# A late layernorm apply moved to ScalarE, and PSUM slots behind the loop taken from a written list

## Chip, cores and metric

The kernel runs on one core of a Trainium2 chip. The engines are PE (TensorE matmuls; PEld are its weight loads), DVE (VectorE), ACT (ScalarE), POOL (GpSimd) and SP (SyncE, which here only issues DMAs). The metric is the device time of one execution in microseconds (us); less is better. The kernel before takes 275.93 us, the median of 3 runs (275.52 to 276.19).

## What is computed

One transformer block on x of 2048 rows and 640 columns in bf16: layernorm, a linear attention with a softmax feature map, a residual, a second layernorm, a gated feed-forward layer of width 1536, and a residual. Cut to what matters:

```python
def _A_ref(x, wqkv, w_phi, wo):            # 32 heads of 20 columns
    q, k, v = qkv[0], qkv[1], qkv[2]       # of x @ wqkv
    phi_q = concat([softmax(q @ w_phi), softmax(-(q @ w_phi))])
    phi_k = concat([softmax(k @ w_phi), softmax(-(k @ w_phi))])
    kv = einsum("bhsf,bhsd->bhfd", phi_k, v)
    z  = einsum("bhsf->bhf", phi_k)
    o  = (phi_q @ kv) / (phi_q . z + 1e-6)
    return o @ wo
def _B_ref(x, w_gate, w_up, w_down):
    return (gelu(x @ w_gate) * (x @ w_up)) @ w_down
h  = x + _A_ref(_layernorm(x), ...)
h2 = h + _B_ref(_layernorm(h), ...)
```

## The kernel before

The 2048 rows are 16 tiles of 128. All of the kernel stands under a manual schedule: each engine runs its instructions in the order of the source, and waits only for what it needs.

**Front (to about 20 us).** The first tiles are normalised and projected, and w_phi is folded into the key weights. Tiles 0 and 1 are a special case (`CT`): what goes into their columns of `LN1T[0]` at first is x less its mean; 1/std is applied later, as the scale of the ScalarE evictions. For tile 1 the list `va[1]` holds four columns: minus the mean (0), the sum of squares (1), the variance plus eps (2) and 1/std (3).

**The loop over 16 passes (lines 463 to 514).** Pass t makes the keys of tile t (`k_tile`: PE into `pk`, two ScalarE exponentials into `E`), the values of tile t+4 (`v_mm`, `v_ev`), the layernorm of tile t+6 (`ln_ap`), and the norm of the keys (`k_norm`: a sum and a reciprocal on DVE, two products `vt`, on POOL and DVE). Passes 10 to 14 also fold w_phi into the query weights (`fold`, PE into `wa`, a ScalarE cast into `Wq2`). Some passes run `kv_tile` for tiles gathered up to then; it adds to `kvp` in PSUM. Since the query matmuls need tiles 0 and 1 normalised in full, their columns of `LN1T[0]` are written once more, by a layernorm and a transposing DMA of SP: tile 1 in pass 10 (`ln_a(1)`, line 396, on DVE) and tile 0 in pass 12 (`ln_ap(0, on_act=True)`, line 144, on ScalarE). Pass 13 has SP issue the loads of `Wo` and `Wg`. Pass 15 makes the first four query groups `q_mm(0..3)` (PE into `pq`, ScalarE exponentials into `Eq`); the first needs tiles 4 to 7 alone, the second is the first to read `LN1T[0]`. Behind the loop `kv_tile(13..15)` ends `kvp`, and `kv_mask` (lines 358 and 360, DVE) writes the masked `KV` from it.

**Behind the loop.** The other query groups `q_mm(q)` to `q_mm(q+8)` (q is 4) are woven by hand with the attention of tiles 0 to 2: `attn_a` (PE into two tiles `ab`, copied out by ScalarE and DVE), `attn_b` to `attn_b3`, `attn_t` and `attn_e` (transposes), `attn_c` (PE into `po`), `attn_d`. Then `weave` runs units of the feed-forward layer (`gate_up`: ten matmuls into `gu`, a gelu on ScalarE from its first half, a product on DVE from its second; `down`: twelve matmuls into `pd`) with pieces of later tiles' attention between them. The first `weave` is of tiles 0 and 1, the second of tiles 2 and 3, and so on.

**PSUM.** The kernel divides PSUM into eight banks. In the loop a pool of three slots of two banks (`psG`, banks 0 to 5) serves `pk`, `pv`, `wa` and `pq` in turn, and `kvp` has the last two banks. The last four tiles of the three slots are the query groups 0 to 3: group 1 in banks 4 and 5, group 2 in banks 2 and 3, group 0 and then group 3 in banks 0 and 1. Behind the loop the pools are closed and `psG2` opens, four slots of two banks. In the kernel as compiled, its 63 tiles get the slots (slot i is banks 2i and 2i+1) 0, 3, 2, 1, 3, 2, 0, 3, 2, 3, 1 and so on, to a last `0, 1, 3, 2, 0, 1, 3, 2`; the first is the `pq` of `q_mm(q)`, the next two are `ab` of tile 0, and the last is the `gu` of the twelfth `gate_up` of the second `weave`. Right behind that unit `split()` closes the pool and opens `psB`, eight slots of one bank, which hand out banks 0, 7, 6, 1, 5, 4, 3, 2; the first is `pd` of the unit that follows, `down(0, 2, 0)`. A pool of eight single-bank slots begins at bank 0 whatever was there before. All these pools are opened with `reuse_waits="tile"`: a new tile waits for all that read the old tile in its place. This goes by whole tiles: in the compiled kernel the `ab` tile in bank 5 behind the split waits for the gelu of the last `gu`, though that gelu reads bank 4 alone.

Of the kernel before, what the change touches and what calls it, by code (L numbers as in the profile page):

```python
# [8 lines left out]
BF16 = mybir.dt.bfloat16  # L9
F32 = mybir.dt.float32  # L10
ALU = mybir.AluOpType
ACTF = mybir.ActivationFunctionType
AX = mybir.AxisListType
PSUM = bass.MemoryType.PSUM
# [3 lines left out]
def kernel(  # L18
# [12 lines left out]
    nc = tc.nc  # L31
    P = 128
# [42 lines left out]
    ps_cm = ExitStack()  # L75
    psG = ps_cm.enter_context(tc.tile_pool(name="psG0", bufs=4, space=PSUM, reuse_waits="tile"))
# [4 lines left out]
    x_sb = [const.tile([P, 4, D], BF16, name=f"x_sb{b}") for b in range(NB)]  # L81
# [19 lines left out]
    def small(pool, shape, name, bufs=3):  # L101
        return pool.tile(shape, F32, name=name, bufs=bufs)

    def gtile(name):
        return psG.tile([P, 2, 512], F32, name=name, tag="G")

    def ln_stats(pool, tiles, tag, act=True, between=None, log=False):

# [43 lines left out]
    def transpose_to(dst, src, on_pe, on_dve=False):  # L152

        if on_pe:
            tp = psG.tile([P, 16, P], BF16, name="tp", tag="G")
            for c in range(NC):
                nc.tensor.transpose(tp[:, c, :], src[:, c * P:(c + 1) * P], ident)  # L157
            (nc.vector.tensor_copy if on_dve else nc.scalar.copy)(dst, tp[:, 0:NC, :])  # L158
        else:
            nc.sync.dma_start_transpose(dst, src)  # L160
# [4 lines left out]
    LN1T = [LN1F.bitcast(BF16).rearrange("p (b c n) -> p b c n", b=NB, c=NC)[:, b] for b in range(NB)]  # L165
# [56 lines left out]
    def fold(WT, W2, quarters, ds=range(NC)):  # L222


        n, w = (2, QF) if quarters else (1, HD)
        runs = []
        for c in range(NC):
            lo, hi = H0[c] * Dh, (H0[c] + NH[c]) * Dh
            for r in range(2 * n):
                a, b = max(lo, r * w), min(hi, (r + 1) * w)  # L230
                if a < b:
                    runs.append((r // n, r, c, a, b))
        runs.sort()
        for d in ds:
            wa = gtile("wa")
            wr = wa.rearrange("p u (q x) -> p (u q) x", q=n)
            for i, (u, r, c, a, b) in enumerate(runs):
                nc.tensor.matmul(wr[:, r, a - r * w:b - r * w], lhsT=WT[:, c, d * P:(d + 1) * P],
                                 rhs=BD[:, c].rearrange("p a b -> p (a b)")[:, a - H0[c] * Dh:b - H0[c] * Dh],
                                 start=(i == 0 or runs[i - 1][0] != u),  # L240
                                 stop=(i + 1 == len(runs) or runs[i + 1][0] != u), skip_group_check=True)
            dst, src = W2[:, d, :].rearrange("p (u f) -> p u f", u=2), wr[:, :, 0:w]
            if quarters:
                dst = W2[:, d, :].rearrange("p (c r f) -> p r c f", c=NC, r=4)
                src = src.rearrange("p r (c f) -> p r c f", c=NC)
            if d in (QA if quarters else KA):
                nc.scalar.copy(dst, src)
            else:
                nc.vector.tensor_copy(dst, src)
# [19 lines left out]
    def ln_ap(t, on_act=False, on_pe=False):  # L269
        ln = (ln_act if on_act else ln_dve)(p1, "1", *lnp[t])  # L270
        if on_pe:
            lnp[t] = ln
        else:
            transpose_to(LN1T[t // 4][:, :, t % 4 * P:(t % 4 + 1) * P], ln, False)
# [15 lines left out]
    def v_mm(t, us=(0, 1)):  # L290
        if 0 in us:
            pv[t] = gtile("pv")
        proj(pv[t], t, Wv, us)
# [10 lines left out]
    def v_ev(t):  # L304
        nc.scalar.activation(vS[t % 8][:, :, 0:Dh].rearrange("p (u h) f -> p u h f", u=2),
                             pv[t][:, :, 0:HD].rearrange("p u (h f) -> p u h f", f=Dh), ACTF.Copy,
                             scale=lnp[t][2] if t in CT else 1.0)
# [5 lines left out]
    def k_tile(t):  # L313
        pk = gtile("pk")
        proj(pk, t, Wk2, rows=t == 0)
        Ek[t] = ev.tile([P, 2, D], BF16, name="E", bufs=8)
        for s in range(2):
            nc.scalar.activation(Ek[t][:, s, :].rearrange("p (u f) -> p u f", u=2), pk[:, :, 0:HD],  # L318
                                 ACTF.Exp, scale=((lnp[t][2], nrstd[t]) if t in CT else (1.0, -1.0))[s])
# [25 lines left out]
    def kv_tile(t):  # L345

        for s in range(2):
            for c in range(NC):
                i, h, n = SLOT[c]
                for r in range(4):  # L350
                    f0, h0 = r * QF + c * 32, r * QH + h
                    nc.tensor.matmul(kvp[QUAD[r], s * SL + i:s * SL + i + n, :],  # L352
                                     lhsT=Ek[t][:, s, f0:f0 + 32], rhs=Vt[t][:, s, h0:h0 + n, :],
                                     start=(s == c == t == 0), stop=(t == NT - 1), skip_group_check=True)
# [10 lines left out]
    def q_mm(j, part=(0, 1)):  # L365

        if 0 in part:
            pqs[j] = gtile("pq")
        for i, bc in enumerate(QG[j]):
            if i not in part:  # L370
                continue
            b, c = divmod(bc, NC)
            for kc in range(NC):
                nc.tensor.matmul(pqs[j][:, i, :], lhsT=Wq2[:, kc, c * P:(c + 1) * P], rhs=LN1T[b][:, kc, :],  # L374
                                 start=(kc == 0), stop=(kc == NC - 1))

    def q_exp(j, signs=(0, 1)):
        for s in signs:
            nc.scalar.activation(Eq[j][:, :, s, :], pqs[j][:, 0:len(QG[j])], ACTF.Exp, scale=(1.0, -1.0)[s])  # L379
# [13 lines left out]
    def ln_a(t):  # L393

        ln = p1.tile([P, D], BF16, name="ln1", bufs=3)
        nc.vector.tensor_scalar(ln, x_sb[0][:, t, :], va[t][:, 0:1], va[t][:, 3:4], op0=ALU.add, op1=ALU.mult)
        return ln

    def xc_a(t):
# [6 lines left out]
    va = {1: p1.tile([P, 4], F32, name="va1")}  # L406
# [56 lines left out]
    for t in range(NT):  # L463
        if t == T3:
            ps_cm.close()
            psG = ps_cm.enter_context(tc.tile_pool(name="psG", bufs=3, space=PSUM, reuse_waits="tile"))
            psK = ps_cm.enter_context(tc.tile_pool(name="psK", bufs=1, space=PSUM, reuse_waits="tile"))
            kvp = psK.tile([P, 2 * SL, VC], F32, name="kvp")
        k_tile(t)
        if t == 0:  # L470
            ln_ap(6)
        if t in FQ:
            fold(WqT, Wq2, True, [i for i, f in enumerate(FQ) if f == t])
        for i in KVG.get(t, ()):
            kv_tile(i)
        for j in range(len(QT)):
            if t == QT[j]:
                q_mm(j)
                q_exp(j)
                for i in KVQ.get(j, ()):  # L480
                    kv_tile(i)
        if 0 < t < NT - 4:
            v_mm(t + 4)
        if t > 0 and t + 6 < NT:
            ln_ap(t + 6, on_act=True)
        if 0 < t < NT - 4:
            v_ev(t + 4)
        if t % 2 == 0 and t + 8 < NT:
            ln_st(t + 8, t + 9)
        k_norm(t)  # L490
        load_T(WqT, 0, *[i for i, f in enumerate(LQ) if f == t])
        if t == 10:
            transpose_to(LN1T[0][:, :, P:2 * P], ln_a(1), False)
        if t == 12:
            ln_ap(0, on_act=True)
        if t == 7:
            nc.gpsimd.memset(kmask[QUAD[0]], 1.0)
            for k, lo, n, base in ((3, 0, 2, 0), (2, 6, 3, 12)):
                m = kmask[QUAD[0], lo:lo + 6].rearrange("p (k n) -> p k n", k=k)
                nc.gpsimd.affine_select(out=m, in_=m, pattern=[[4, k], [-Dh, n]],  # L500
                                        compare_op=ALU.is_ge, fill=0.0, base=base, channel_multiplier=1)
                nc.gpsimd.affine_select(out=m, in_=m, pattern=[[-4, k], [Dh, n]],
                                        compare_op=ALU.is_ge, fill=0.0, base=Dh - 1 - base, channel_multiplier=-1)
        if t == 8:
            nc.gpsimd.memset(KV, 0.0)
        if t == 9:
            for r in (1, 2, 3):
                nc.sync.dma_start(kmask[QUAD[r]], kmask[QUAD[0]])
        if t == 11:
            nc.gpsimd.tensor_copy(KV[:, 0, :, KC - 1], kmask)  # L510
            nc.gpsimd.tensor_copy(KV[:, 1, :, 0], kmask)
        if t == 13:
            nc.sync.dma_start(Wo, wo_v)
            nc.sync.dma_start(Wg, wg_v)
# [5 lines left out]
    p1_cm.__exit__(None, None, None)  # L520
    ps_cm.close()
    ps_cm = ExitStack()
    psG = ps_cm.enter_context(tc.tile_pool(name="psG2", bufs=4, space=PSUM, reuse_waits="tile"))


    p2 = ctx.enter_context(tc.tile_pool(name="p2", bufs=1, reuse_waits="tile"))
# [334 lines left out]
```

## Time and profile before

| | us |
|---|---|
| median of 3 runs (lowest, highest) | 275.93 (275.52, 276.19) |
| the profiled execution, its own time | 276.65 |
| its span, first to last instruction | 274.7 |
| PE busy in the span | 268.2 |
| DVE, ACT, POOL busy | 174.2, 141.1, 96.6 |

The profile is of one execution, which took 276.65 us; its instructions span 274.7, and 1.95 lie around them. The granted TensorE clock was 0.999 of full speed. A timeline row has start, length, engine (`SPq` is SP's queue), line, operation, tiles as out<-in, shapes and a count; several like instructions that follow one another are one row. What stands in brackets is the engine's idle time ahead of the row and what ended it.

### The profile page before, as it was taken

How to read it: one execution, taken by the hardware profiler on the slowest of the kernel's cores; microseconds unless marked ns; L12 is line 12 of the kernel's file. 1: busy time of each engine (PE TensorE's matmuls, PEld its weight loads, DVE VectorE, ACT ScalarE, POOL GpSimd, SP SyncE). 2: the span in 40 equal slices, each digit the busy share in tenths (PEclk: the TensorE clock that was granted, in tenths of full speed). 3: DMA queues.
4: the chain of work that ended last, by engine and by line, in shares of the span. 5: the costliest groups of instructions: out<-in, count | busy, mean ns of one | idle time of the engine just before them, and what ended most of it. 6: DMA issues, size and time to landing. Idle time of an engine off the chain costs nothing.

```text
span 274.7 us, 7230 instructions
## 1 busy us (share of the span) xinstructions
PE 268.2 (98%) x2978; PEld 171.7 (63%) x2995; DVE 174.2 (63%) x332; ACT 141.1 (51%) x241; POOL 96.6 (35%) x219
## 2 busy tenths in 40 slices
PE   7999999999899999999999999999999999999996
PEld 4776777774455887788754554675554576444574
DVE  5879999997586776675459873346976333333332
ACT  5789897787689755374534445212445510223100
POOL 4248999775012227365321552101165300000000
PEclk9999999999999999999999999999999999999999
DMA  7963637577079021323111232110214111000011
GB/s 190 221 218 71 66 60 91 78 152 312 2 246 328 5 50 37 85 51 73 33 43 49 26 70 51 40 58 1 66 32 64 35 48 50 24 0 0 2 48 48
DMA packets 42400, 21.46 MB, mean 78 GB/s; under 512 B 35200, under 2 KB 40576, under 8 KB 42368
## 3 DMA queue, kind: packets, MB, share of 16 engines
q1 hardware_dynamic: 41712, 20.98, 31.9%
q8 instruction: 23, 0.38, 0.6%
q10 hardware_dynamic: 656, 0.03, 0.2%
q14 instruction: 9, 0.07, 0.1%
HBM read 10.18 MB, written 2.62 MB: 47 GB/s over the span
## 4 chain that ended last, share of the span: by engine, by line
PE 73%; issue 0%; ACT 0%; DVE 0%
PE gu L697 38%; PE pd L716 19%; PE po L637 8%; PE pq L374 5%; PE ab L565 2%; PE tp L157 0%; ACT Eq L379 0%; DVE y L719 0%
## 5 line engine op out<-in xcount | busy, mean ns | idle before, releaser
L703 DVE TENSOR_TENSOR GT<-gu,g 128x512 bf16<-128x512 f32 (+1 forms) x60 | 34.4, 580 | 47.3 <-PE gu L697 38.5
L700 ACT ACTIVATE g<-gu 128x512 bf16<-128x512 f32 (+1 forms) x60 | 30.7, 512 | 63.6 <-PE gu L697 62.7
L697 PE MATMUL gu<-LN2T,Wg 128*128 128x512 bf16 (+1 forms) x289 | 61.2, 335 | 0.6
L697 PE MATMUL gu<-LN2T,Wu 128*128 128x512 bf16 (+1 forms) x300 | 61.8, 336 | 0.0
L716 PE MATMUL pd<-Wd,GT 128*128 128x320 bf16 (+2 forms) x396 | 53.5, 295 | 0.0
L716 PEld LDWEIGHTS <-GT 128*128 128x128 bf16 x396 | 37.9, 98 | 14.6 <-DVE GT L703 0.2
L697 PEld LDWEIGHTS <-Wu 128*128 128x128 bf16 x300 | 29.4, 98 | 22.6
L697 PEld LDWEIGHTS <-Wg 128*128 128x128 bf16 x300 | 28.6, 98 | 20.8
L285 PEld LDWEIGHTS <-LN1T 128*128 128x128 bf16 x290 | 27.7, 98 | 11.2 <-DMA LN1T<-ln 0.9
L719 DVE TENSOR_TENSOR y<-pd,x_sb 128x320 bf16<-128x320 f32 (+2 forms) x29 | 13.9, 480 | 29.4 <-PE pd L716 29.4
L333 POOL TENSOR_TENSOR vt<-vS,rs 128x672 bf16<-128x672 bf16 x22 | 29.2, 1349 | 7.5 <-DVE rs L329 7.2
L637 PE MATMUL po<-Wo,oT 128*128 128x320 bf16 x160 | 24.4, 299 | 0.0
L285 PE MATMUL pk<-Wk,LN1T 128*128 128x320 bf16 x160 | 24.2, 299 | 0.0
L374 PE MATMUL pq<-LN1T,Wq 128*128 128x512 bf16 x94 | 22.9, 379 | 1.2 <-ACT Eq L379 0.9
L325 DVE TENSOR_REDUCE sk<-E 128x64 f32<-128x1280 bf16 x16 | 22.9, 1430 | 0.0
L379 ACT ACTIVATE Eq<-pq 128x1024 bf16<-128x1024 f32 (+1 forms) x26 | 20.0, 828 | 3.3 <-PE pq L374 3.3
L285 PE MATMUL pv<-Wv,LN1T 128*128 128x320 bf16 x130 | 19.8, 299 | 0.4 <-DMA LN1T<-ln 0.3
L637 PEld LDWEIGHTS <-oT 128*128 128x128 bf16 x160 | 15.5, 98 | 7.0 <-ACT oT L158 0.5
L318 ACT ACTIVATE E<-pk 128x640 bf16<-128x640 f32 x28 | 18.2, 706 | 3.0 <-PE pk L285 2.9
L614 DVE TENSOR_TENSOR tt<-AB,w 128x1280 bf16<-128x1280 f32 x12 | 17.8, 1486 | 1.0 <-POOL w L607 0.9
L144 ACT ACTIVATE ln<-x_sb,v,rstd 128x640 bf16<-128x640 bf16 x14 | 12.9, 920 | 10.8 <-POOL v L676 10.3
L374 PEld LDWEIGHTS <-Wq 128*128 128x128 bf16 x100 | 9.4, 98 | 10.6 <-PE kvp L352 0.5
(114 smaller groups left out, 288.7 us busy)
## 6 DMA issues: line engine op xcount, KB each, us to landing
out_dram<-y SPq DMA_DIRECT2D x15, 160.0 KB, 1.8
Wg<-in_B_w_gate_dram SPq DMA_DIRECT2D x1, 1920.0 KB, 10.2
Wu<-in_B_w_up_dram SPq DMA_DIRECT2D x1, 1920.0 KB, 8.5
Wd<-in_B_w_down_dram SPq DMA_DIRECT2D x2, 960.0 KB, 11.8
x_sb<-in_A_x_dram SPq DMA_DIRECT2D x2, 640.0 KB, 6.5
Wo<-in_A_wo_dram SPq DMA_DIRECT2D x1, 800.0 KB, 5.6
x_sb<-in_A_x_dram SPq DMA_DIRECT2D x4, 160.0 KB, 3.4
Wv<-in_A_wqkv_dram SPq DMA_DIRECT2D x2, 320.0 KB, 4.5
```

The costliest lines, as they stand in the source:

```text
L285: nc.tensor.matmul(ps[:, u, 0:HD], lhsT=lnT(t, c), rhs=W[:, c, u * HD:(u + 1) * HD], start=(c == 0), stop=(c == NC - 1))
L318: nc.scalar.activation(Ek[t][:, s, :].rearrange("p (u f) -> p u f", u=2), pk[:, :, 0:HD], ACTF.Exp, scale=((lnp[t][2], nrstd[t]) if t in C ...
L325: nc.vector.reduce_sum(sk, Ek[t].rearrange("p s (h f) -> p (s h) f", f=Dh), axis=AX.X)
L333: eng.tensor_tensor(vt[:, s], vS[t % 8], rs[:, s * H:(s + 1) * H, None].to_broadcast([P, H, VC]), ALU.mult)
L374: nc.tensor.matmul(pqs[j][:, i, :], lhsT=Wq2[:, kc, c * P:(c + 1) * P], rhs=LN1T[b][:, kc, :], start=(kc == 0), stop=(kc == NC - 1))
L379: nc.scalar.activation(Eq[j][:, :, s, :], pqs[j][:, 0:len(QG[j])], ACTF.Exp, scale=(1.0, -1.0)[s])
L614: nc.vector.tensor_tensor(tt.rearrange("p s (h f) -> p s h f", f=Dh), num, w[:, :, :, None].to_broadcast([P, 2, H, Dh]), ALU.mult)
L637: nc.tensor.matmul(pos[u], lhsT=st[t][:, c, :], rhs=Wo[:, c, u * HD:(u + 1) * HD], start=(c == 0), stop=(c == NC - 1))
L697: nc.tensor.matmul(gu[i][:, 0:n], lhsT=W[:, c, f * P:(f + 1) * P], rhs=LN2T[b][:, c, a0:a1], start=(c == 0), stop=(c == NC - 1))
L700: nc.scalar.activation(g[:, 0:n], gu[0][:, 0:n], ACTF.Gelu_apprx_tanh)
L703: nc.vector.tensor_tensor(st[b, "g", f][:, a0:a1], gu[1][:, 0:n], g[:, 0:n], ALU.mult)
L716: nc.tensor.matmul(ps, lhsT=st[b, "g", f][:, tl * P:(tl + 1) * P], rhs=Wd[:, f, f0:f1], start=(f == 0), stop=(f == NF - 1))
```

## The change

`ln_a(1)` goes from DVE to ScalarE and, with its transposing DMA, from pass 10 to pass 13, ahead of that pass's loads of `Wo` and `Wg`. ScalarE's form needs minus the mean times 1/std as a bias; one POOL multiply in pass 8 puts it into `va[1][:, 2:3]`. Behind the loop four pools of one slot each take the place of the pool of four, and a written list `ROT` says which of them each tile gets.

```diff
-    def gtile(name):
-        return psG.tile([P, 2, 512], F32, name=name, tag="G")
+    psP = None
+
+    def gtile(name, shape=[P, 2, 512], dt=F32):
+        return (psP[ROT.pop(0)] if psP else psG).tile(shape, dt, name=name, tag="G")
...
-            tp = psG.tile([P, 16, P], BF16, name="tp", tag="G")
+            tp = gtile("tp", [P, 16, P], BF16)
...
         ln = p1.tile([P, D], BF16, name="ln1", bufs=3)
-        nc.vector.tensor_scalar(ln, x_sb[0][:, t, :], va[t][:, 0:1], va[t][:, 3:4], op0=ALU.add, op1=ALU.mult)
+        nc.scalar.activation(ln, x_sb[0][:, t, :], ACTF.Identity, bias=va[t][:, 2:3], scale=va[t][:, 3:4])
         return ln
...
-        if t == 10:
-            transpose_to(LN1T[0][:, :, P:2 * P], ln_a(1), False)
         if t == 12:
             ln_ap(0, on_act=True)
+        if t == 13:
+            transpose_to(LN1T[0][:, :, P:2 * P], ln_a(1), False)
...
         if t == 8:
+            nc.gpsimd.tensor_tensor(va[1][:, 2:3], va[1][:, 0:1], va[1][:, 3:4], op=ALU.mult)
             nc.gpsimd.memset(KV, 0.0)
...
-    psG = ps_cm.enter_context(tc.tile_pool(name="psG2", bufs=4, space=PSUM, reuse_waits="tile"))
+    psP = [ps_cm.enter_context(tc.tile_pool(name=f"psP{i}", bufs=1, space=PSUM, reuse_waits="tile")) for i in range(4)]
+    ROT = [2, 3, 0, 1, 3, 0, 2, 3, 0, 3, 1, 3, 1, 2, 0, 3, 1, 0, 2, 3, 0,
+           1, 2, 3, 0, 1, 2, 0, 1, 3, 2, 0, 1, 2, 3, 0, 1, 2, 3, 0, 1, 2,
+           3, 0, 1, 3, 0, 2, 1, 3, 0, 2, 1, 3, 0, 2, 1, 3, 0, 2, 1, 3, 0]
```

`ROT` has 63 entries. Entry by entry it is the order in which `psG2` hands out its slots in the kernel before, with 0 written for 2 and 2 for 0.

## Prediction

> **What bounds the kernel now.** I read the busy times first: PE 268.2 of 274.7 us, DVE 174.2, ACT 141.1. So a change counts by what it does to PE's gaps. Next the waits of PE itself from 20 us on:
>
> ```profile
> PE pq L374 <- ACT Eq L379: 0.9, 1, 0.9
> PE pv L285 <- DMA LN1T<-ln: 0.3, 1, 0.3
> ```
>
> The reader is to see that PE waits twice for other engines after the first 20 us. The 0.3 is a transpose near 47 us, which the change leaves alone. The 0.9 stands at the end of the loop, and the timeline there shows it whole:
>
> ```profile
> 62.07 1.14 PE L352 MATMUL kvp<-vt,E 128*32 128x42 bf16 x120
> ...
> 63.14 5.57 PE L374 MATMUL pq<-LN1T,Wq 128*128 128x512 bf16 x24
> ...
> 65.51 1.94 ACT L379 ACTIVATE Eq<-pq 128x1024 bf16<-128x1024 f32 x2 [1.40 <-PE pq L374]
> ...
> 67.67 2.92 ACT L379 ACTIVATE Eq<-pq 128x1024 bf16<-128x1024 f32 x4 [0.22 <-PE pq L374]
> ...
> 68.64 1.14 PE L352 MATMUL kvp<-vt,E 128*32 128x42 bf16 x120
> ...
> 70.09 0.68 DVE L360 TENSOR_TENSOR KV<-kvp,kmask 128x504 bf16<-128x504 f32 x1
> 70.23 0.10 PEld L374 LDWEIGHTS <-Wq 128*128 128x128 bf16 x1 [0.55 <-PE kvp L352]
> 70.64 1.24 PE L374 MATMUL pq<-LN1T,Wq 128*128 128x512 bf16 x4 [0.86 <-ACT Eq L379]
> ...
> 71.81 0.47 PE L565 MATMUL ab<-KV,Eq 32*128 32x44 bf16 x40
> ```
>
> The first pq behind the loop sits in slot 0, where query group 3 was; it starts at 70.64, 0.05 after the last exponential of that group (67.67 + 2.92 = 70.59). From there PE runs on without a wait to the end (the chain of waits is PE's own from 70.64), and DVE, ACT and POOL follow it. So a time won or lost on PE here is kept, until PE meets a new wait. The place for one is the split, where the pool of eight single banks opens:
>
> ```profile
> 132.92 0.71 PE L697 MATMUL gu<-LN2T,Wu 128*128 128x256 bf16 x5
> ...
> 133.35 0.76 ACT L700 ACTIVATE g<-gu 128x256 bf16<-128x256 f32 x2
> ...
> 133.46 3.42 PE L716 MATMUL pd<-Wd,GT 128*128 128x320 bf16 x24
> ...
> 133.75 0.81 DVE L703 TENSOR_TENSOR GT<-gu,g 128x256 bf16<-128x256 f32 x2 [1.37 <-ACT g L700]
> ```
>
> The reader is to see the order: PE begins pd at 133.46, right behind the last gu, while that gu is still to be read, by ACT until 133.35 + 0.76 = 134.11 and by DVE until 133.75 + 0.81 = 134.56.
>
> **The layernorm: off DVE.** Line 396 goes, at 51.85 a row of 1.00 us. DVE's products then come up to 1.0 earlier, and PE doesn't wait for DVE or POOL in the loop: 0.
>
> The Trainium skill ("ScalarE: Activation LUTs", section "Rules for kernel authors") speaks against this move: adds and multiplies belong on VectorE, not on ScalarE. The rows say the same by half: the same shape takes 0.445 on DVE at line 149, but 1.00 in this place, and 0.94 on ACT. By the rule the move would cost 0.5 us, by the rows of this place it costs none; in the sum it is neither, since neither engine holds PE here.
>
> **The layernorm: onto ACT.** The nearest row is tile 0's, of the same shape one pass before:
>
> ```profile
> 54.57 0.70 ACT L247 CAST Wq<-wa 128x640 bf16<-128x640 f32 x1
> 55.14 0.94 ACT L144 ACTIVATE ln<-x_sb,mrc,rstdc 128x640 bf16<-128x640 bf16 x1
> 55.96 1.31 ACT L318 ACTIVATE E<-pk 128x640 bf16<-128x640 f32 x2
> 57.13 0.72 ACT L247 CAST Wq<-wa 128x640 bf16<-128x640 f32 x1
> 58.33 1.30 ACT L318 ACTIVATE E<-pk 128x640 bf16<-128x640 f32 x2 [0.47 <-PE pk L285]
> ```
>
> A cast gives way to the layernorm after 55.14 - 54.57 = 0.57, and that to the next exponentials after 55.96 - 55.14 = 0.82. The new one starts at 57.13 + 0.57 = 57.70, and pass 14's exponentials at 58.52 instead of 58.33: of 0.82 the idle 0.47 and its edges hide all but about 0.2. Behind them wait the cast of pass 14, pass 15's exponentials and, for its PSUM slot, the first pq of pass 15. PE begins that at 59.82; the exponentials end at 58.33 + 1.30 = 59.63, now 59.83, and with the handover of 0.05 pq starts at 59.88: +0.06. Later ACT work of the loop waits for PE (0.76 idle before the next Eq). Ends: 0, if the cover is whole, and 0.2, if ACT's delay reaches PE in full. I take +0.06.
>
> The transpose goes along. SP runs in order: tile 0's leaves at about 56.11, as now; tile 1's when ACT is done, 57.70 + 0.94 = 58.64, and ends on SP at about 59.9; Wo and Wg go out behind it at about 59.9 and 61.0 instead of 57.37 and 58.46, each 2.5 later. Issue to landing took 2.6 in the median and 4.6 at most for these transposes, so tile 1 lands at 61.3, at most 63.3. PE first reads LN1T[0] in the second pq of pass 15, at 63.14 + 0.06 = 63.20: 1.9 of cover, or 0.1 late. I take 0. Wo lands 5.6 after its issue, at 65.5, and is read at 79.48; Wg 10.2 after, at 71.2, read at 90.04: no cost.
>
> The POOL multiply of pass 8 has no row of its own; 128x1 operations on POOL take 0.19 to 0.57. It stands ahead of a row before which POOL idles 0.85: 0 at either end.
>
> **The slots at the loop's end.** The list puts the first pq into slot 2, where group 1 was: its exponentials end at 65.51 + 1.94 = 67.45, long before. How soon PE then follows on kvp is seen where a kvp block is followed by pq without a wait: 62.07 to 63.14, 1.07. So pq starts at 68.64 + 1.07 = 69.71 instead of 70.64: **-0.93**. What is late next: ab needs KV, written until 70.09 + 0.68 = 70.77, and its second tile now sits in slot 0, free at 70.59. PE comes to ab 71.81 - 70.64 = 1.17 after the start of pq, at 70.88: 0.1 behind KV, so no new wait. All three move by the 0.06 alike. The later entries keep every tile's neighbour, 0 and 2 being exchanged throughout. Least gain: the weights of this pq load only at 70.23, 0.41 before its matmul, and no row says why; if that isn't the slot's doing, pq can't start before 70.23 and the gain is 0.41.
>
> The skill ("TensorE: Matmul & The Clock Gate", section "Step-by-step: what each phase is for") says that weight loads are pulled ahead of running matmuls. By the rule the load should have come at 69.7 and the gain is 0.93; the row at 70.23, if it is no effect of the wait, gives 0.41.
>
> **The slots at the split.** The last entry was 2 and is 0. So the last gu, till now in banks 4 and 5, is in banks 0 and 1, and bank 0 is what the new pool hands out first, to pd. Before, pd found there a po that DVE had read by 131.21 + 0.08 = 131.29, over 2 us earlier. Now it must wait for both readers of the gu: until 134.56, plus the handover of 0.05, 134.61, against 133.46: **+1.15**. Queued behind it on PE is everything to the end. Ends: 134.11 + 0.05 - 133.46 = 0.70, if only ACT's half of the gu counts, and 0, if pd isn't in bank 0. I take 1.15, since before already a tile in bank 5 waits for the reader of bank 4.
>
> **Sum**, against the profiled execution of 276.65 us (span 274.7): 0.06 - 0.93 + 1.15 = +0.28, so 276.93. The median of the runs shown is 275.93, 0.72 below that execution; the same difference gives 276.21, a ratio of 1.001. Within 0.2% is 0.55 us here, about what a measurement of this kernel can tell from no change. So: **no change that counts**, two larger things that cancel.
>
> **Rivals.**
> - Faster: the split costs nothing. For it: the wait isn't in the trace of before, only worked out from the slots. Against it: the list's last entry, and that the banks are handed out from 0. It gives 0.06 - 0.93 = -0.87, 275.06. With ACT's half alone it is -0.17, 275.76, still no change.
> - Slower: the weight load of 70.23 is bound by something else, such as the end of the dense kvp block (its last matmuls end at 69.78). Place: the first pq behind the loop. Price: 0.52 less gain, so 0.06 - 0.41 + 1.15 = +0.80, 276.73. It decides from the point where this load starts later than 70.0. Against it: at 63.14 load and matmul follow kvp at once.
> - Slower: the transpose of tile 1 lands late, pushed by the 2.7 MB of Wo and Wg behind it. If it took the 6.5 of the x loads in the front, it would land at 65.2, and PE would wait 2.0: +2.3, 278.2. Against it: tile 0's transpose, with the same loads right behind it, cost PE nothing.
> - It doesn't do what it says: if the four pools don't lie in the order of the list, both slot effects vanish: +0.06, 275.99, no change.
>
> **How the numbers follow.** Chances: the forecast 0.50, its own range 276.0 to 276.6 (loop 0 to 0.2, the gain and the stall 0.1 each); no stall 0.17; half the stall 0.08; weight load 0.15; late transpose 0.05; no slot effect 0.05. Faster: the 0.17 and 0.02 of scatter from the half stall, 0.19. Slower: 0.15 and 0.05, and 0.10 of the forecast, whose upper end passes 276.48: 0.30. Same: the rest, 0.51. The range reaches from the rival without a stall, 275.06, to the weight load's 276.73, with a little for the scatter of medians: 275.0 to 276.9; outside it are the late transpose and the tails.
>
> **What would show it.** Right: no idle time of PE between kvp and pq near 69.7 and ab at about 70.9; a new wait of PE, pd for DVE's GT, of about 1.15 near 133.7; ACT's layernorm at 57.7 and pass 14's exponentials at 58.5; SP's transpose at 58.7, landed before 63. Wrong: pd starts right behind gu (then faster by 0.87); the weight load still half a us behind kvp; PE waiting for LN1T near 63.

## The result, and the profile after

| | before | after |
|---|---|---|
| median (lowest, highest), 7 runs each, side by side | 276.40 (275.52, 276.97) | 277.73 (277.41, 278.14) |
| ratio to before, 95% interval | 1 | 1.0054 [1.004, 1.0067] |
| the profiled execution, its span | 276.65, 274.7 | 277.65, 275.9 |

The change made the kernel slower by about 0.5%. The forecast was no change that counts, 276.21 in a range of 275.0 to 276.9; the time lies above that range. First the waits of PE in the kernel after (what waited, for whom, us in total, times, longest):

```profile
PEld L376 <- issue: 1.7, 1, 1.7
...
PE pq L376 <- ACT Eq L381: 1.6, 1, 1.6
...
PE pd L722 <- DVE GT L709: 1.0, 1, 1.0
```

The reader is to see two things. The wait of pd for the gu's reader is new, as forecast. And the wait at the loop's end, which the list of slots was to remove, has grown from 0.9 to 1.6. The timeline of the kernel after shows the loop's end:

```profile
66.99 2.92 ACT L381 ACTIVATE Eq<-pq 128x1024 bf16<-128x1024 f32 x4 [0.22 <-PE pq L376]
67.97 1.14 PE L354 MATMUL kvp<-vt,E 128*32 128x42 bf16 x120
...
69.41 0.68 DVE L362 TENSOR_TENSOR KV<-kvp,kmask 128x504 bf16<-128x504 f32 x1
70.74 0.76 PEld L376 LDWEIGHTS <-Wq 128*128 128x128 bf16 x5 [1.74 <-issue]
70.75 1.25 PE L376 MATMUL pq<-LN1T,Wq 128*128 128x512 bf16 x4 [1.65 <-ACT Eq L381]
71.93 0.46 PE L571 MATMUL ab<-KV,Eq 32*128 32x44 bf16 x40
```

The label names the exponentials, but it can't be right. The last of them end at 66.99 + 2.92 = 69.91, 0.84 before pq starts, and they read group 3, which no longer shares pq's slot. KV is written by 70.09. Nothing that pq needs ends near 70.74. The row above says more: now the weight load comes together with its matmul, and what it waited for is "issue", that is, nothing that the profile shows. In the kernel before the load stood alone at 70.23.

The split, in the same timeline:

```profile
133.03 0.71 PE L703 MATMUL gu<-LN2T,Wu 128*128 128x256 bf16 x5
...
133.46 0.76 ACT L706 ACTIVATE g<-gu 128x256 bf16<-128x256 f32 x2
...
133.87 0.81 DVE L709 TENSOR_TENSOR GT<-gu,g 128x256 bf16<-128x256 f32 x2 [1.37 <-ACT g L706]
...
134.73 1.52 PE L722 MATMUL pd<-Wd,GT 128*128 128x320 bf16 x10 [0.99 <-DVE GT L709]
```

pd starts 0.05 after 133.87 + 0.81 = 134.68: the worked-out wait, in its place. From the start of the last gu matmul to pd it is 1.26, where before it was 0.11: +1.15.

So what held pq? A row of the page that the prediction did not read, in the list of DMA queues, beside the counts of part 1:

```profile
PE 268.8 (97%) x2978; PEld 172.2 (62%) x2995; DVE 173.5 (63%) x331; ACT 141.5 (51%) x242; POOL 97.0 (35%) x220
...
q8 instruction: 23, 0.38, 0.5%
```

A queue that carries instructions moved 0.38 MB in 23 packets, 16 KB each. Only PE has a program of that size: 2,995 weight loads and as many matmuls (2,978 of them on record in this trace), about 260 instructions to a packet. The packets' times are in the trace's DMA records; a packet lands when its transfer ends. In the kernel after, one of them starts at 68.17 and lands at 69.20, and pq's weight load starts 1.54 later. In the kernel before, it is 67.54 and 68.63, and the load at 70.23 starts 1.60 later. The DMA view of the kernel after from 56 to 72 us (40 slices of 0.4; DMA is the mean busy share of the 16 DMA engines) shows what else was under way:

```profile
DMA  2599030099041499999999999999998111000001
...
q8 instruction: 4, 0.07, 1.7%
...
Wg<-in_B_w_gate_dram SPq DMA_DIRECT2D x1, 1920.0 KB, 10.7
Wo<-in_A_wo_dram SPq DMA_DIRECT2D x1, 800.0 KB, 6.3
```

The engines are full from about 62 to 68.4 with Wo and Wg, and the packet that the theory below gives to pq is fetched at the end of that stretch.

**Theory (packet, or block, theory).** PE's program comes in 16 KB packets; the first pq behind the loop is the first instruction of one; the packet is late because Wo and Wg fill the DMA engines, and PE stands until about 1.5 us after its landing. Before, this wait and that for the slot ended within 0.4 of one another (70.23 and 70.59), so taking one away left the other; and the moved transpose pushes Wo and Wg, and with them the packet, later. **Rival (slot theory).** The label is right: a slot or an exponential holds pq. A third reading, that the dense kvp block holds the weight load, is told apart by the same runs.

### The profile page after: what moved, and what is told of

Its sections match the earlier page's. It is cut to its first block, busy times and chain, and to the rows that moved or that the text cites. A ratio compares the mean times of both kernels' runs of the same rounds, so it can differ in the third digit from the quotient of the medians.

```text
span 275.9 us, 7231 instructions
## 1 busy us (share of the span) xinstructions
PE 268.8 (97%) x2978; PEld 172.2 (62%) x2995; DVE 173.5 (63%) x331; ACT 141.5 (51%) x242; POOL 97.0 (35%) x220
## 4 chain that ended last, share of the span: by engine, by line
PE 72%; ACT 1%; issue 1%; DVE 0%; ACTq 0%
PE gu L703 37%; PE pd L722 19%; PE po L643 8%; PE pq L376 5%; PE ab L571 2%; PE tp L159 0%; ACT ln L146 0%; DVE GT L709 0%; ACT sq L673 0%; ACT Eq L381 0%; ACT g L706 0%; DVE y L725 0%; ACTq L673 0%; ACTq L706 0%
```

## Experiments

Times of one profile are set against one another by three stretches of PE: up to the start of the last kvp matmul (this moves from profile to profile, with the transposes of the front), from there to the second ab matmul (the second, since in run 5 PE waits between the first and the second), and from there to the end. "First" is the start of the first instruction of the packet in question, "lag" the time from the packet's landing to it.

| kernel | packet landed | first | lag | kvp to ab | ab to end | median | ratio to before |
|---|---|---|---|---|---|---|---|
| before | 68.63 | 70.23 | 1.60 | 2.22 | 202.84 | 276.40 | 1 |
| after | 69.20 | 70.74 | 1.54 | 3.02 | 203.99 | 277.73 | 1.0054 [1.004, 1.0067] |
| slots only | 68.34 | 69.83 | 1.49 | 2.11 | 204.02 | 276.71 | 1.0025 [1.0015, 1.0036] |
| layernorm only | 69.46 | 70.88 | 1.42 | 2.72 | 202.86 | 276.68 | 1.0023 [1.0011, 1.0034] |
| after, last five slots changed | 69.36 | 70.68 | 1.32 | 2.90 | 203.27 | 276.97 | 1.0037 [1.0024, 1.005] |
| after, last 17 slots changed | 69.85 | 71.34 | 1.49 | 3.15 | 202.84 | 276.66 | 1.0027 [1.0011, 1.0043] |
| after, 12 instructions fewer | 69.42 | 70.96 | 1.54 | 1.78 | 204.03 | 276.72 | 1.0012 [1.0, 1.0023] |
| after, 16 instructions more | 70.18 | 71.59 | 1.41 | 1.31 | 203.99 | 277.57 | 1.0035 [1.0021, 1.005] |
| after, late loads | 66.06 | 70.29 | 4.24 | 1.31 | 203.99 | 276.10 | 0.9997 [0.9983, 1.001] |
| before, late loads | 64.95 | 68.79 | 3.84 | 2.22 | 202.85 | 276.11 | 0.9985 [0.9973, 0.9997] |
| slots only, last 17 changed | 68.02 | 69.42 | 1.40 | 1.77 | 202.85 | 275.54 | 0.9995 [0.9975, 1.0015] |
| after, last 17 changed, late loads | 65.45 | 69.38 | 3.93 | 1.31 | 202.83 | 275.04 | 0.9948 [0.9931, 0.9965] |
| the same without the layernorm move | 65.31 | 68.99 | 3.68 | 1.31 | 202.83 | 275.04 | 0.9961 [0.9945, 0.9978] |

(Each ratio is against runs of before on the same chip; those had medians of 276.06 to 276.40. So rows are compared by their ratios, not by their medians.)

**1. The slots only.** The kernel before with the four pools and `ROT`; the layernorm as it was.

```diff
-    psG = ps_cm.enter_context(tc.tile_pool(name="psG2", bufs=4, space=PSUM, reuse_waits="tile"))
+    psP = [ps_cm.enter_context(tc.tile_pool(name=f"psP{i}", bufs=1, space=PSUM, reuse_waits="tile")) for i in range(4)]
+    ROT = [2, 3, 0, 1, 3, 0, 2, 3, 0, 3, 1, 3, 1, 2, 0, 3, 1, 0, 2, 3, 0,
...
```

> The kernel before with the written slot list alone; the layernorm of tile 1 stays on DVE in pass 10. Block theory: the first pq behind the loop is the first instruction of a 16 KB block of PE's program, and what holds it is the load of that block, which comes late while Wo and Wg are in flight. Then taking the slot wait away lets pq start only when its block is there, near 70.2 as its weight load did before: 0.4 gained, 1.15 lost at the split, +0.7 us, ratio about 1.003. Slot theory (the profile's own releaser, ACT's exponentials): pq starts at 69.7, 0.93 gained, 1.15 lost, +0.2, ratio 1.001.

Its timeline at the loop's end:

```profile
66.98 2.92 ACT L381 ACTIVATE Eq<-pq 128x1024 bf16<-128x1024 f32 x4 [0.22 <-PE pq L376]
...
69.83 0.76 PEld L376 LDWEIGHTS <-Wq 128*128 128x128 bf16 x5 [0.84 <-PE kvp L354]
69.83 1.25 PE L376 MATMUL pq<-LN1T,Wq 128*128 128x512 bf16 x4 [0.74 <-PE kvp L354]
```

pq starts at 69.83, before the exponentials of group 3 end at 69.90, so the slot no longer holds it. Yet PE stood, until 1.49 after the packet's landing. Of the 0.91 that a kernel with neither wait gains (2.22 to 1.31 in the table), 0.11 is left here, and the wait at the split costs 1.18. The ratio of 1.0025 is 0.7 us.

**2. The layernorm only.** The other half: line 396 on ScalarE, `ln_a(1)` with its transpose in pass 13, the POOL multiply; the old pool.

```diff
-        if t == 10:
-            transpose_to(LN1T[0][:, :, P:2 * P], ln_a(1), False)
...
+        if t == 13:
+            transpose_to(LN1T[0][:, :, P:2 * P], ln_a(1), False)
```

> The kernel before with the move of tile 1's layernorm to ScalarE and pass 13 alone; slots as before. Block theory: the transpose of tile 1 now stands ahead of the loads of Wo and Wg, which leave 1.4 to 1.9 later, so PE's block lands later too and pq starts at about 70.75 instead of 70.64: +0.1, ratio 1.000 to 1.002, with the weight load of that pq no longer ahead of its matmul. Rival, that the layernorm itself costs time on ACT: pass 14's exponentials 0.2 later, the first pq of pass 15 0.06 later, the end +0.06. Rival, slot theory: pq again 0.05 behind the last exponential of group 3.

```profile
67.43 2.92 ACT L379 ACTIVATE Eq<-pq 128x1024 bf16<-128x1024 f32 x4 [0.22 <-PE pq L374]
68.40 1.14 PE L352 MATMUL kvp<-vt,E 128*32 128x42 bf16 x120
...
70.88 0.76 PEld L374 LDWEIGHTS <-Wq 128*128 128x128 bf16 x5 [1.44 <-issue]
70.89 1.25 PE L374 MATMUL pq<-LN1T,Wq 128*128 128x512 bf16 x4 [1.34 <-ACT Eq L379]
```

Here the slot is the old one, and its exponentials end at 67.43 + 2.92 = 70.35; pq starts 0.54 later, and 1.43 after the packet's landing. Wo and Wg leave SP at 59.62 and 60.26, as in the kernel after (59.25, 59.89), where the kernel before has 57.37 and 58.46. So the layernorm move, which by itself touches nothing at the loop's end, lengthens the stretch from kvp to ab by 0.50 through the packet alone. That is more than the 0.1 expected, and the ratio of 1.0023 lies just above the 1.000 to 1.002 expected. The two halves make 0.0025 + 0.0023 = 0.0048 of the 0.0054.

**3. The kernel after with the last five slots changed**, so that the last gu is in slot 2.

```diff
-           3, 0, 1, 3, 0, 2, 1, 3, 0, 2, 1, 3, 0, 2, 1, 3, 0, 2, 1, 3, 0]
+           3, 0, 1, 3, 0, 2, 1, 3, 0, 2, 1, 3, 0, 2, 1, 3, 2, 0, 1, 3, 2]
```

> The changed kernel with the last five entries of the slot list 2, 0, 1, 3, 2 instead of 0, 2, 1, 3, 0, so that the last gu before the split is in slot 2 and pd finds bank 0 free. Split theory: the wait of pd for DVE's GT goes, 1.15 us less than the changed kernel, so +0.1 to +0.4 against the kernel before, ratio 1.000 to 1.0015. Rival, that pd waits for the GT it reads and not for its bank: the wait stays, ratio 1.005.

The wait of pd is gone (gu to pd 0.11), but its waits list has a new row:

```profile
PE gu L703 <- DVE GT L709: 0.3, 1, 0.3
```

Slot 2 now comes back after three tiles instead of four, and its reader isn't done: 0.43 in the stretch from ab to the end (203.27 against 202.84). The net gain there is 0.72, and the split term is confirmed. The wait of pq stays, 1.71 from kvp. The ratio of 1.0037 is above the 1.000 to 1.0015 expected: the new wait was not foreseen, and that pq's wait stays is not in that sum.

**4. The kernel after with late loads.** Wo and Wg are held until group 2's exponentials are done, by a POOL copy of one column into each, which reads that group's `Eq`.

```diff
-        if t == 13:
-            nc.sync.dma_start(Wo, wo_v)
-            nc.sync.dma_start(Wg, wg_v)
...
+    nc.gpsimd.tensor_copy(Wo[:, 0, 0:1], Eq[2][:, 0, 1, 0:1])
+    nc.sync.dma_start(Wo, wo_v)
+    nc.gpsimd.tensor_copy(Wg[:, 0, 0:1], Eq[2][:, 0, 1, 0:1])
+    nc.sync.dma_start(Wg, wg_v)
```

> The changed kernel with the loads of Wo and Wg held back until the exponentials of query group 2 are done (a POOL copy of one column into each, then the load; about 69 us instead of 59). Block theory: no load is in flight when PE's block is fetched, its packet starts near 65 instead of 68.2, pq follows kvp at once (69.0 to 69.2), ab waits for KV at about 70.1 to 70.3; 0.8 to 1.6 less than the changed kernel, ratio against before 0.9995 to 1.0025 (the 1.15 of the split stays). Slot theory and the theory that PE needs a pause behind the dense kvp block: pq starts near 70.7 as in the changed kernel, ratio 1.005.

The packet lands at 66.06, 4.24 ahead of its use, and pq follows kvp at once (0.12 from matmul to matmul). The wait at the split stays. That its span (275.5) is only 0.4 below the kernel after's has a cause in the front: this profile has two waits for `LN1T`, 1.1 in all, and kvp ends 1.25 later than in the kernel after.

**5. Twelve PE instructions fewer.** The kernel after, with the eight warm-up matmuls of 128 columns at the start made two of 512. The columns are the same; all that follows stands 12 places earlier in PE's program.

```diff
-    warm(*[512] * 7, *[P] * 8)
+    warm(*[512] * 9)
```

> The kernel after, but the eight warm-up matmuls of 128 columns at the start are two of 512: the same columns, 12 fewer TensorE instructions, nothing else moved. Every later instruction stands 12 places earlier in TensorE's program, so the bound between its 16 KB packets, which in the kernel after lies exactly ahead of the first pq behind the loop, now lies behind the five pq matmuls and the first ab. Packet theory: pq starts within 0.2 us of the last kvp matmul (about 69.0 instead of 70.75); the wait comes back at the second or third ab, about 1.5 us behind the packet's landing, near 70.7; ab so starts about 1.2 earlier than in the kernel after (71.93), and the ratio to before falls from 1.0054 to about 1.001. Rival, a slot or an exponential holds pq (what the profile's releaser says): pq stays at 70.7, 1.6 behind the last kvp, and the ratio stays near 1.005. The wait at the split stays at 1.1 to 1.2 in both.

```profile
68.24 1.14 PE L354 MATMUL kvp<-vt,E 128*32 128x42 bf16 x120
...
69.31 1.25 PE L376 MATMUL pq<-LN1T,Wq 128*128 128x512 bf16 x5
...
70.49 0.19 PE L571 MATMUL ab<-KV,Eq 32*128 32x44 bf16 x1
70.96 0.36 PEld L571 LDWEIGHTS <-Eq 32*128 32x128 bf16 x39 [0.38 <-issue]
70.96 0.46 PE L571 MATMUL ab<-KV,Eq 32*128 32x44 bf16 x39 [0.28 <-issue]
```

This is the run that decides. pq now follows kvp at once, with the same slots and the same exponentials. The five pairs of pq and the first pair of ab are 12 instructions, and behind just these PE stands, until 1.54 after the packet's landing. A bare count of instructions moved the wait; no slot, exponential or array state goes by that count. The ratio of 1.0012 is the one expected.

**6. Sixteen instructions more**, by the same matmuls cut smaller.

```diff
-    warm(*[512] * 7, *[P] * 8)
+    warm(*[512] * 7, *[64] * 16)
```

> The opposite of the last: the eight warm-up matmuls of 128 columns are sixteen of 64, the same columns and 16 more TensorE instructions. The bound between packets now lies 16 instructions ahead of the first pq, eight matmuls before the end of kvp. Packet theory: the wait of about 1.6 us stands inside kvp, before its last eight matmuls, and pq follows the last kvp within 0.2 us; the ratio to before stays near 1.005. Rival, a slot or an exponential holds pq: kvp runs through and pq waits 1.6 us behind it as in the kernel after.

```profile
69.16 1.07 PE L354 MATMUL kvp<-vt,E 128*32 128x42 bf16 x112
71.59 0.12 PEld L354 LDWEIGHTS <-E 128*32 128x32 bf16 x8 [1.47 <-issue]
71.60 0.23 PE L354 MATMUL kvp<-vt,E 128*32 128x63 bf16 x8 [1.36 <-issue]
...
71.76 0.76 PEld L376 LDWEIGHTS <-Wq 128*128 128x128 bf16 x5
71.76 1.25 PE L376 MATMUL pq<-LN1T,Wq 128*128 128x512 bf16 x5
```

The wait now stands inside kvp, eight pairs, that is 16 instructions, before its end, and pq has none. With the last run this closes the rival and the third reading. The ratio of 1.0035 is below the 1.005 expected. (This profile is of the longest of eight executions and has a wait of PE of 1.3 for ACT near 28 us.)

**7. Both waits taken away.** The kernel after with late loads as in 4, and slots 0 and 2 exchanged through the last seventeen entries. Where the exchange begins, slot 0 comes back after four tiles instead of three, and slot 2 after five instead of six; behind that every slot keeps its distance.

```diff
-           3, 0, 1, 3, 0, 2, 1, 3, 0, 2, 1, 3, 0, 2, 1, 3, 0, 2, 1, 3, 0]
+           3, 0, 1, 3, 2, 0, 1, 3, 2, 0, 1, 3, 2, 0, 1, 3, 2, 0, 1, 3, 2]
```

> The kernel after with both of its waits taken away: slots 0 and 2 exchanged through the last seventeen entries of the list, so that the last gu is in slot 2 and no slot comes back sooner than it did; and the loads of Wo and Wg held until group 2's exponentials are done, so that no load is under way when the packet of the first pq is fetched. Packet theory with the split term: pq follows kvp at once (-1.65 against the kernel after), pd follows the last gu at once (-1.15), so up to 2.8 below the kernel after: ratio to before 0.994 to 0.997, time 274.6 to 275.5, less what a late transpose costs by chance. Rival, the wait is a slot's or an exponential's: pq stays 1.6 behind kvp and the ratio is about 1.001.

The timeline at the two places, and the DMA view from 56 to 69.4 us:

```profile
68.32 1.14 PE L354 MATMUL kvp<-vt,E 128*32 128x42 bf16 x120
...
69.39 1.25 PE L376 MATMUL pq<-LN1T,Wq 128*128 128x512 bf16 x5
...
131.67 0.71 PE L704 MATMUL gu<-LN2T,Wu 128*128 128x256 bf16 x5
...
132.22 3.42 PE L723 MATMUL pd<-Wd,GT 128*128 128x320 bf16 x24
```

```profile
DMA  0049900310598020000000000100000000000000
...
q8 instruction: 3, 0.05, 1.4%
```

Against the DMA row of the kernel after, the stretch from 62 to 68.4 is empty but for packets of instructions (the digit 1 at 64.4 is the packet of pq). Both waits are gone, and the kernel beats both: 275.04, 0.35 to 0.69% below before.

**8. The kernel before with late loads alone.**

```diff
-            nc.sync.dma_start(Wo, wo_v)
-            nc.sync.dma_start(Wg, wg_v)
...
+    nc.gpsimd.tensor_copy(Wo[:, 0, 0:1], Eq[2][:, 0, 1, 0:1])
+    nc.sync.dma_start(Wo, wo_v)
...
```

> The kernel before with one edit, the loads of Wo and Wg held until group 2's exponentials are done. Packet theory: the packet lands early, but the slot of pq is still held by group 3's last exponentials, which end near 70.5, so pq stays near 70.6 and the ratio is 0.998 to 1.001: in the kernel before the two waits ended within 0.4 of one another. If the slot had held nothing there, pq would come to about 69.7 and the ratio to 0.9965.

```profile
66.75 2.92 ACT L379 ACTIVATE Eq<-pq 128x1024 bf16<-128x1024 f32 x4 [0.22 <-PE pq L374]
67.72 1.04 PEld L352 LDWEIGHTS <-E 128*32 128x32 bf16 x120 [0.42 <-issue]
...
68.79 0.10 PEld L374 LDWEIGHTS <-Wq 128*128 128x128 bf16 x1
...
69.72 1.24 PE L374 MATMUL pq<-LN1T,Wq 128*128 128x512 bf16 x5 [0.86 <-ACT Eq L379]
```

With the packet early, the weight load comes at 68.79, right behind kvp, and only the matmul waits, until 0.05 after the exponentials end at 69.67. This is the slot's wait by itself, and the stretch from kvp to ab is the same 2.22 as before. So in the kernel before two waits lay on top of one another, and the load at 70.23 was the mark of the second.

**9. The same as 7 without the layernorm move** (against 7; the POOL multiply goes too):

```diff
-        nc.scalar.activation(ln, x_sb[0][:, t, :], ACTF.Identity, bias=va[t][:, 2:3], scale=va[t][:, 3:4])
+        nc.vector.tensor_scalar(ln, x_sb[0][:, t, :], va[t][:, 0:1], va[t][:, 3:4], op0=ALU.add, op1=ALU.mult)
...
+        if t == 10:
+            transpose_to(LN1T[0][:, :, P:2 * P], ln_a(1), False)
...
-        if t == 13:
-            transpose_to(LN1T[0][:, :, P:2 * P], ln_a(1), False)
```

> The kernel before with the list of slots (slots 0 and 2 exchanged through its last seventeen entries) and the late loads of Wo and Wg, but tile 1's layernorm left where it was, on VectorE in pass 10. If the layernorm move in itself is worth nothing, as the prediction had it (+0.06, 0 to 0.2), this is the same as the last run of this sort with the move in it: ratio 0.994 to 0.996, pq at once behind kvp, pd at once behind the last gu. If the move brought time of its own, the ratio is 0.997 or more; if it cost some, 0.993 or less.

The stretches behind the loop are those of 7 to 0.01. The medians are the same 275.04, but on two chips; the ratios, 0.9948 with the move and 0.9961 without, have intervals that overlap. So no gain and no cost of the move shows in the time. The traces show a small cost ahead of the loop's end: from the first pk matmul of pass 15 to the first pq it is 1.36 in all five kernels with the layernorm on DVE and 1.44 to 1.45 in all nine with it on ACT, 0.09 more.

**10. The kernel after with the last seventeen entries exchanged**, loads as they are.

```diff
-           3, 0, 1, 3, 0, 2, 1, 3, 0, 2, 1, 3, 0, 2, 1, 3, 0, 2, 1, 3, 0]
+           3, 0, 1, 3, 2, 0, 1, 3, 2, 0, 1, 3, 2, 0, 1, 3, 2, 0, 1, 3, 2]
```

> The kernel after with slots 0 and 2 exchanged through the last seventeen entries of the list, nothing else. Split term: pd follows the last gu within 0.2 us and no gu waits for a slot before it, so the run is 1.15 below the kernel after: ratio to before 1.001, 276.4 to 276.8. The wait of pq behind the loop stays at 1.3 to 1.8 us, about 1.5 behind the packet's landing, by the packet theory. If the split's wait were not the slot's (the activation of the last gu itself is late), pd stays 1.1 late and the ratio 1.005.

The split's wait is gone without a new one (202.84). The packet wait is 1.96 from kvp to pq in this profile, 0.13 more than in the kernel after, and the ratio of 1.0027 lies above the 1.001 expected; its interval reaches down to 1.0011.

**11. The slots alone with the last seventeen entries exchanged**: what the written list is worth with the loads where they were. Against run 1:

```diff
-           3, 0, 1, 3, 0, 2, 1, 3, 0, 2, 1, 3, 0, 2, 1, 3, 0, 2, 1, 3, 0]
+           3, 0, 1, 3, 2, 0, 1, 3, 2, 0, 1, 3, 2, 0, 1, 3, 2, 0, 1, 3, 2]
```

> The kernel before with the list of slots alone, slots 0 and 2 exchanged through its last seventeen entries; loads and layernorm stay where they were. This is the slots alone (ratio 1.0025) less the wait at the split (1.15 us, 0.0042): 0.9983, between 0.997 and 1.000. At the loop's end the packet theory still has pq wait until about 1.5 us behind the packet's landing, near 70, so that only a part of the 0.93 that the list was to bring there is seen; if the packet held nothing, pq would follow kvp at once and the ratio would be 0.9955 or less.

pq starts 1.40 after the packet's landing and 0.58 after the last kvp, so half of the 0.91 shows in this profile, and 0.11 in run 1: it goes by when the packet lands. The ratio of 0.9995 can't be told from no change; it is above the 0.9983 expected and inside its range.

**12. The kernel after with tile 1's transpose behind the loads**, an attempt to bring Wo and Wg back to their old time.

```diff
-        if t == 13:
-            transpose_to(LN1T[0][:, :, P:2 * P], ln_a(1), False)
...
             nc.sync.dma_start(Wg, wg_v)
+            transpose_to(LN1T[0][:, :, P:2 * P], ln_a(1), False)
```

> The kernel after with tile 1's transpose issued behind the loads of Wo and Wg instead of ahead of them. The loads then start near 57 as in the kernels without the layernorm move. Packet theory: the packet of the first pq behind the loop starts about 1 us earlier against the entry of the block before (1.0 instead of 2.2). But the first pq of the loop waits for tile 1's transpose, which now lies behind 2.7 MB of loads: it lands 3 to 9 us late, and the whole run is 2 to 8 us longer, ratio 1.007 to 1.03. If the transpose passes the loads, the ratio is 1.002 to 1.003, as with the slots alone.

The median is 285.91, ratio 1.0338 [1.0305, 1.0371]. Its waits of PE, and its busy times in two stretches (busy us of the engines, then the granted clock of PE, DMA share, GB/s):

```profile
PE pq L376 <- DMA LN1T<-ln: 7.0, 1, 7.0
```

```profile
60.00:69.00 9.00, 2.50 (x127) 1.50 (x125) 6.14 (x7) 2.78 (x4) 4.60 (x3) 0.83 1.07 316
69.50:73.00 3.50, 3.50 (x10) 1.22 (x11) 0.00 (x0) 0.00 (x0) 0.00 (x0) 0.54 0.02 5
```

The transpose lands behind the loads, and PE waits 7.0 for it. The ratio is past the range expected, and the clock has a part in that: after the idle time it was 0.54 in the mean of the next 3.5 us, and the pq matmuls from there to the last kvp took 7.13 instead of the kernel after's 5.57. The packet of the pq behind the loop started at 70.82, 3.7 ahead of PE's entry into the packet before it and not 1.0 behind that entry, as was expected; this pq follows kvp at once. So the order of the change, transpose first, is the right one of the two; the loads are what has to move.

## Why the prediction was wrong, point by point

- **What bounds the kernel: right.** PE's gaps at the two places named make the whole difference from the end of the loop on: from ab to the end the kernels differ by the split alone.
- **The layernorm off DVE and onto ACT, +0.06: right.** From pass 15's keys to its first pq it is 0.09 more with the move, the place named and nearly the size (run 9). That the first pq of pass 15 starts at 59.15 in the kernel after, where it was 59.82, is no gain: that profile was ahead by 0.76 at pass 11 already (its keys start at 48.01 instead of 48.77), and so was that of run 1, which is without the move.
- **"Wo and Wg go out behind it ... each 2.5 later ... no cost": the step that failed.** The times were nearly right (59.25 and 59.89 issued, 65.58 and 70.57 landed), and their readers do have the cover that was claimed. But the loads were asked only about their own readers. While they are under way, PE's packet comes late, and later still when they leave later: +0.50 by run 2, and 0.91 (3.02 - 2.11) on top of the slots, where the prediction had 0.
- **"The slots at the loop's end ... -0.93": the mechanism was right, the gain was not there to be had.** A slot did hold pq (run 8), and with the packet out of the way the gain is 2.22 - 1.31 = 0.91. But the packet ends its wait nearly as late: -0.11 in run 1, and in the change as a whole +0.80. By the two profiles the sum, 0.06 - 0.93 + 1.15, should have had 0.09 + 0.80 + 1.15 = 2.04. Less the 0.76 by which the profile of after was ahead this is 1.28, the difference of the spans (275.93 - 274.66 = 1.27); it has to be, since the stretches make up the span. The medians differ by 1.33, so 0.7 of the 2.04 doesn't show in them.
- **The least gain of 0.41, and the rival of the weight load at +0.80: the right row, priced too low.** The prediction saw that no row says why the weights load only at 70.23, and gave this 0.15. Two things were missing: that the load is the beginning of a packet that comes later while large loads are under way, so that 70.23 is no fixed bound; and that the other half of the change moves it. The argument against the rival, that load and matmul follow kvp at once at 63.14, holds only where no packet begins.
- **The slots at the split, +1.15: right**, 1.15 measured, in its place and with its releaser; run 10 takes it away whole.
- **The rival of a late transpose: not in this change**, but run 12 shows the mechanism, at 7.0.

Two rules of the Trainium skill can now be set beside rows. "TensorE: Matmul & The Clock Gate", section "Step-by-step: what each phase is for", says that weight loads are pulled ahead. Run 8 agrees, with the load 0.93 ahead of its waiting matmul; the 70.23 of the kernel before was, by the packet theory, no exception to the rule, as the load had not yet been fetched. And "Runtime: NRT & Kernel Launch", section "Instruction fetch mechanics", says that an engine's program is refilled in blocks of 16 KiB, 256 instructions, and that crossing a block is mostly hidden. The 23 packets of 16 KB agree, and so does a wait that moves by 12 and 16 places with the count; "mostly hidden" holds where the packet landed 3.7 to 4.2 before its use, and not here, where under 400 GB/s of loads it cost PE up to 1.8.

**What stays open.** When a packet is asked for isn't in the trace, so whether it waits in the DMA engines behind the loads or is asked for late is not shown; only that without the loads it lands 2.7 to 4.4 us earlier in the four pairs of kernels that differ in this. Its own transfer takes as long with the loads (0.9 to 1.2) as without (0.9 to 1.1), so it starts later and is not moved more slowly. Nor is it shown why it starts about 1.2 later when `Wo` leaves about 2.6 later (67.08 to 67.54 in the three profiles with the layernorm on DVE and the loads in pass 13, 68.17 to 68.76 in five with it on ACT), or what the 1.5 between landing and first instruction goes to. By their ratios the four kernels with late loads come out 0.2 to 0.5 below what their stretches alone would give against the profile of before, and the kernel after comes out lower too, as said. Both would follow for the most part if the packet held PE some 0.2 to 0.5 longer in most executions of the kernel before than in the profiled one; that is an estimate from these differences, and no trace shows it.

## What to carry to other kernels

Where a weight load that should run ahead stands alone and late, and the profile gives "issue" or a releaser that had long ended, look at the instruction queue's packets in the trace before you book a gain: a second wait may lie right under the one you remove. A large load that is moved is to be asked about more than the readers of its data: here it held up the program of the engine that sets the end. And a list of slots is to be followed past its end: here the last tile's bank was the first that the next pool handed out, and a swap at the end alone shortened a slot's distance (0.43), while a swap carried through cost nothing (202.84).

## What the runs showed of the hardware that was not expected

- For PE's program of 5,990 weight loads and matmuls, 23 packets of 16 KB were moved within the span, and PE stood still at the beginning of one until 1.32 to 1.60 after its landing, in all nine profiles where it came late.
- With 2.7 MB of loads at about 400 GB/s under way, the packet landed 1.3 to 1.6 before its use and PE waited; without, 3.7 to 4.2 before, and no wait.
- Twelve instructions fewer at the start, of the same columns, took 1.24 us (3.02 to 1.78) from a stretch 65 us later, 0.4% by the ratios.
- After 7 us without matmuls the granted clock was 0.54 in the mean of the next 3.5 us.
